# Softcap attention into a maxout MLP on one core: the second pair's k and q as f32 on the hardware queues, w_out first on GpSimd's queue, w1 in column halves

## The chip, the core and the metric

The kernel runs on one core of one Trainium2 chip. The core has five engines that work side by side, each through its own list of instructions in order: TensorE (PE: matmuls; PEld is its loading of weights), VectorE (DVE), ScalarE (ACT), GpSimd (POOL) and SyncE (SP). They wait for one another by semaphores. Data moves between the chip's main memory and the on-chip memory SBUF by DMA, which SyncE, ScalarE and GpSimd can issue; matmuls write to the accumulator memory PSUM. The metric is device time in microseconds (us) of one execution; lower is better.

## What is computed

```python
def _attn_ref(q, k, v, cap):                      # (8, 12, 448, 64) each, cap 30
    scale = 1.0 / np.sqrt(q.shape[-1])
    scores = scale * np.matmul(q, k.transpose(0, 1, 3, 2))
    scores = cap * np.tanh(scores / cap)
    scores = scores - np.max(scores, axis=-1, keepdims=True)
    attn = np.exp(scores)
    attn = attn / (np.sum(attn, axis=-1, keepdims=True) + 1e-09)
    return np.matmul(attn, v)

def _moe_ref(x, w1, w2, w_out):                   # x (3584, 768), w1, w2 (768, 1024), w_out (1024, 768)
    h1 = x @ w1
    h2 = x @ w2
    g = np.maximum(h1, h2)
    return g @ w_out
```

`x` is the attention's result with the heads side by side. All inputs and the output are f32.

## The kernel before

**Two pairs of formulas.** The maxout is rewritten as max(h1, h2) = relu(x (w1 - w2)) + x w2, so the result is relu(x wd) w_out + x wm with wd = w1 - w2 (`wd_sb`) and wm = w2 w_out (`wm_sb`). Both are made in the kernel, at its start: wd by subtractions on VectorE (step `sub`, L390), wm by "premultiplying" (`P`, L419), for which w2 is first turned by TensorE (`W`, L404) and copied out of PSUM (`WC`, L408).

**Attention, by pairs of heads.** The 8 x 12 heads make 48 pairs. The first ten pairs' k and q arrive as rows in `kqs` (two buffers of two pairs each), are turned by 28 transposes of 64 x 64 on TensorE (`X`, or `Xh` for one of its halves; L446) and copied to `qkT` (`XC`, L451). From pair 10 on a DMA transposes them (`cr`). Scores of a pair are three matmul groups (`S i j`, L502) into one of two score tiles in PSUM, s0 and s1; ScalarE takes the tanh out of them (`T`, L507) and then the exponential in SBUF (`E`, L524). The last 64 columns of two pairs share one tile (`L`, `TL`, `EL`). Sums of the exponentials (`Y`), their inverses (`Y1` to `Y3`) and the products with v (`VL`, `V`, L588 and L594) give `xT` (`N`, L606 and L609).

**The MLP.** 120 groups of matmuls (`M x y n`, L633) take `xT` with `wd_sb` (stage one, relu on VectorE, `ev`) and `xT`, `gT` with `wm_sb`, `wo_sb` (stage two), then the output is stored (`st`). A step of `M` works on two groups at once, one in each half of the array's rows; with -1 one half stays empty.

**The order of everything** is one list of steps, written out by hand or by a planner in the string `ORDER`; each step emits its instructions to their engines in that order, and nothing reorders them. So the order of each engine is the order of its steps in the list. `D bank n` is a filler: ceil(n / 4) matmuls of up to 512 columns on a tile of zeros (`warm`, L459), whose result is never read.

**The loads.** Only pair 0's k and q come as f32 over the hardware queues, k on SyncE's and q on ScalarE's (`ld0`, L303) and are cast to bf16 in `kqs`, k by VectorE, q by ScalarE (`cd`, L308 and L310). All others are cast on the way by GpSimd's DMAs: `lk`, `lq` (L321, one k or q of a pair), `lw2 c` (L370, one of six pieces of w2), `lwo half part` (L364, a quarter of w_out: one half of its columns, one half of its rows), `lv` (L352). `lw1 c` (L370) brings a piece of w1 in f32. Pieces 0 to 3 of w1 go to the output tiles `osb`, 4 and 5 to the second buffer of `xT`; w2 lies in the memory that `gT` takes later. GpSimd's DMAs use eight semaphores in turn, and each DMA waits until the one that last used its semaphore, the eighth before it, has landed.

**The lines that matter at the start**: fillers L459, transposes L446, scores L502 on TensorE; casts L308, L310; tanh L507; GpSimd's `identity` (L277), which writes the identity matrix that transposes need, over a tile that VectorE sets to zero (`ms0`).

Of the kernel before, what the change touches and what calls it, by code (L numbers as in the profile page):

```python
# [15 lines left out]
P 1 0 1; P 2 0 1; P 1 0 2; P 2 0 3; P 0 0 1; P 1 0 1; P 0 0 2; P 1 0 1; PC 2 0; EL 0; TL 1; E 1 0 2; T 2 0; EL 1;  # L16
S 3 0; S 2 2; T 3 0; T 2 2; Y 0 0; S 3 1; X 4 2; VL 0; V 0 1 0 2; V 0 0 0 3; V 0 1 2 3; P 0 0 1; T 3 1; E 2 0 3;
E 3 0 2; Y1 0; Y2 0; XC 4; PC 1 0; Y3 0; N 0 0; N 0 1; PC 0 0; OP 2 1 2; P 2 1 1; OP 0 1 1; P 0 1 4; OP 1 1 0;
P 1 1 1; P 2 1 1; P 1 1 1; P 2 1 2; P 1 1 2; S 3 2; S 4 0; P 0 1 1; P 1 1 1; P 0 1 3; P 1 1 1; OP 3 0 3; P 3 0 1;
P 2 1 1; P 3 0 1; P 1 1 2; T 3 2; T 4 0; E 3 2 3; PC 0 1; PC 1 1; S 4 1; S 4 2; X 5 1; Y 1 0; T 4 1; T 4 2; XC 5;  # L20
Y1 1; lk 8 0; lk 6 0; lq 8 0; lv 1 0; lq 7 0; lq 6 0; lw2 4; lw1 4; lv 5 2; lw1 0; lk 9 0; lw1 2; lv 2 1; lv 5 3;
lq 9 0; lv 2 0; L 2; P 2 1 1; W 5 1; VL 1; V 1 1 0 1; V 1 0 0 3; V 1 1 1 3; TL 2; E 4 0 3; S 5 0; X 6 0; P 2 1 2;
T 5 0; Y2 1; WC 5; Y3 1; N 1 0; N 1 1; PC 2 1; XC 6; P 3 0 4; S 5 1; S 5 2; P 3 0 1; OP 3 1 2; P 3 1 2; P 3 0 1;
W 4 0; P 3 1 4; EL 2; T 5 2; T 5 1; E 5 2 3; E 5 0 2; P 3 1 1; S 6 1; S 6 0; PC 3 0; WC 4; sub 4 0; T 6 1; T 6 0;
X 7 3; OP 4 0 0; P 4 0 5; P 3 1 1; lk 11 1; lw1 5; lw1 1; lw1 3; lv 3 1; lk 10 0; lv 3 0; lq 10 0; lk 10 1;
lk 11 0; lq 11 0; XC 7; sub 0 0; PC 3 1; P 4 0 1; Y 2 3; L 3; P 4 0 2; S 6 2; TL 3; T 6 2; Y1 2; Y2 2; Y3 2;
PC 4 0; sub 2 0; OP 5 0 3; P 5 0 3; S 7 0; X 8 2; X 9 0; VL 2; V 2 1 0 3; V 2 0 0 3; T 7 0; E 6 0 3; XC 9; XC 8;
N 2 1; N 2 0; sub 5 0; S 7 1; P 5 0 2; OP 5 1 2; P 5 1 2; OP 4 1 0; P 4 1 1; P 5 0 3; P 4 1 2; P 5 1 2; O 0 1;
M 0 -1 1; S 7 2; T 7 1; E 7 0 2; T 7 2; PC 5 0; sub 1 0; sub 3 0; S 8 0; P 5 1 4; P 4 1 4; S 8 1; O 1 3; M 1 -1 1;
T 8 0; T 8 1; M 1 -1 2; S 8 2; M 0 -1 5; L 4; Hs 0; cr 5; T 8 2; EL 3; TL 4; E 7 2 3; M 1 0 3; P 4 1 1; PC 5 1;  # L30
A 3 0 1; A 3 1 1; A 3 0 2; B 3 0; B 3 1; PC 4 1; A 3 1 2; VL 3; O 2 2; M 2 0 3; S 9 0; V 3 0 0 2; V 3 1 0 3;
V 3 0 2 3; Y 3 0; M 2 1 3; ev 0; Y1 3; Y2 3; Y3 3; Hs 2; T 9 0; EL 4; E 8 0 3; S 9 1; O 3 0; M 3 1 3; M 3 2 3;
O 4 1; M 4 2 1; Hs 3; M 4 2 2; M 4 3 3; ev 1; N 3 1; ev 2; N 3 0; T 9 1; E 9 0 2; Hs 4; O 5 3; M 5 3 3; M 5 4 3;
O 6 2; M 6 4 3; S 9 2; S 10 0; Hs 5; T 9 2; T 10 0; E 9 2 3; ev 3; M 6 5 3; Hs 6; O 7 0; M 7 5 3; M 7 6 3; S 10 1;
lq 12 0; lq 13 0; lk 13 1; lv 5 0; lk 12 0; lv 4 1; lk 12 1; lv 4 0; lv 5 1; lk 13 0; ev 4; A 4 0 1; A 4 0 2;
A 4 1 1; ev 5; Hs 7; cr 6; O 8 1; M 8 6 3; M 8 7 3; S 10 2; O 9 3; M 9 7 3; H 8; B 4 0; B 4 1; A 4 1 2; ev 6;
ev 7; T 10 1; T 10 2; M 9 8 2; L 5; VL 4; V 4 0 0 3; V 4 1 0 3; Y 4 2; TL 5; E 10 0 3; M 9 8 3; S 11 0; M 9 8 6;
O 10 0; M 10 8 3; Y1 4; Y2 4; Y3 4; N 4 1; N 4 0; Hs 9; Hs 8 2; T 11 0; EL 5; M 10 9 3; M 8 9 1; S 11 1; M 8 9 5;
S 11 2; M 8 9 2; lk 15 1; lq 14 0; lq 15 0; lk 14 0; lv 6 1; lk 14 1; lk 15 0; lv 6 0; lk 16 1; lk 16 0; lk 17 0;
lv 6 3; lv 6 2; lq 16 0; T 11 1; T 11 2; E 11 0 2; O 11 2; M 11 9 3; S 12 0; A 5 0 1; A 5 0 2; ev 8; ev 9;  # L40
M 11 10 7; S 12 1; lk 17 1; M 11 10 4; T 12 0; lq 17 0; O 12 1; M 12 10 1; A 5 1 1; M 12 10 1; Hs 11; cr 7;
M 12 10 1; M 12 11 1; B 5 0; M 12 11 1; T 12 1; M 12 11 1; S 12 2; H 10 2; B 5 1; M 10 11 1; T 12 2; M 10 11 5;
E 11 2 3; st 0 0; M 10 11 2; O 13 3; M 13 11 1; ev 10; L 6; VL 5; A 5 1 2; TL 6; V 5 0 0 2; V 5 1 0 2; Y 5 0;
# [16 lines left out]
TL 8; V 7 0 0 2; V 7 1 0 2; Y 7 3; E 16 0 3; V 7 0 2 3; lk 22 0; V 7 1 2 3; Y1 7; S 17 0; M 22 23 1; lv 9 0;  # L60
M 22 23 1; Y2 7; M 22 23 2; Y3 7; M 22 23 1; lv 9 1; M 22 23 2; O 25 3; M 25 23 1; N 7 0; M 25 23 1; lv 9 2;
# [20 lines left out]
O 38 3; M 38 36 1; A 10 1 1; M 38 36 1; Hs 37; cr 12; M 38 36 1; T 22 1; M 38 37 1; S 22 2; B 10 0; M 38 37 2;  # L82
T 22 2; O 39 2; M 39 37 1; ev 36; M 39 37 2; H 38; B 10 1; E 21 2 3; M 39 38 3; ev 37; L 11; VL 10; TL 11;
# [5 lines left out]
lq 29 0; M 41 40 1; T 24 0; M 41 40 1; A 11 1 1; O 42 3; M 42 40 1; cr 13; M 42 40 2; H 41; B 11 0; T 24 1;  # L89
M 42 41 1; S 24 2; M 42 41 2; H 40 2; B 11 1; M 40 41 1; T 24 2; M 40 41 5; st 2 0; E 23 2 3; M 40 41 2; O 43 2;  # L90
# [15 lines left out]
M 53 52 2; A 13 1 1; M 53 52 2; cr 15; M 53 52 1; T 28 1; M 53 52 1; B 13 0; S 28 2; M 53 52 2; B 13 1; O 54 3;  # L106
M 54 52 1; T 28 2; M 54 52 2; H 53; M 54 53 1; H 52 2; E 27 2 3; M 54 53 2; M 52 53 1; L 14; VL 13; A 13 1 2;
TL 14; V 13 0 0 2; V 13 1 0 2; Y 13 2; E 28 0 3; V 13 0 2 3; lk 34 0; V 13 1 2 3; Y1 13; S 29 0; M 52 53 1;
lv 15 0; M 52 53 1; Y2 13; M 52 53 2; Y3 13; M 52 53 1; lv 15 1; M 52 53 2; O 55 2; M 55 53 1; N 13 0; M 55 53 1;
lv 15 2; M 55 53 1; T 29 0; M 55 54 1; N 13 1; M 55 54 2; lv 15 3; M 55 54 2; EL 14; M 55 54 1; S 29 1; lk 34 1;  # L110
M 55 54 2; ev 52; M 55 54 1; T 29 1; S 29 2; lq 34 0; M 55 54 1; ev 53; M 55 54 1; O 56 0; M 56 54 1; T 29 2;
# [94 lines left out]
def kernel(  # L206
# [165 lines left out]
    def load_w2(c):  # L372
        load_rows(nc.gpsimd, w2b[:, c, :], moe_w2, c)
# [397 lines left out]
```

## Time and profile before

| what | us |
|---|---|
| median of 3 runs | 329.75 (329.73 to 330.23) |
| the profiled execution, device time | 330.89 |
| its span, first to last instruction | 329.1 |
| TensorE busy | 321.2 (98%) |
| ScalarE busy | 280.6 (85%) |
| VectorE busy | 240.5 (73%) |
| GpSimd busy | 161.6 (49%) |
| queue 0 (GpSimd's DMAs), 25.25 MB, share of 16 engines' span | 78.5% |
| queue 1 (SyncE's DMAs), 19.77 MB | 31.1% |

The page divides the span into 40 slices; TensorE's granted clock is full in all of them (mean 0.997). A busy TensorE isn't a TensorE at its peak, since ends of matmuls are modelled and fillers count as busy. Idle time of an engine in a row of the timeline stands in brackets with what ended it. A row such as "4.19 0.56 ACT L310 CAST" gives the start and the length in us, the engine, the line and the operation.

### The profile page before, as it was taken

How to read it: one execution, taken by the hardware profiler on the slowest of the kernel's cores; microseconds unless marked ns; L12 is line 12 of the kernel's file. 1: busy time of each engine (PE TensorE's matmuls, PEld its weight loads, DVE VectorE, ACT ScalarE, POOL GpSimd, SP SyncE). 2: the span in 40 equal slices, each digit the busy share in tenths (PEclk: the TensorE clock that was granted, in tenths of full speed). 3: DMA queues.
4: the chain of work that ended last, by engine and by line, in shares of the span. 5: the costliest groups of instructions: out<-in, count | busy, mean ns of one | idle time of the engine just before them, and what ended most of it. 6: DMA issues, size and time to landing. Idle time of an engine off the chain costs nothing.

```text
span 329.1 us, 9769 instructions
## 1 busy us (share of the span) xinstructions
PE 321.2 (98%) x4136; PEld 184.3 (56%) x4138; DVE 240.5 (73%) x422; ACT 280.6 (85%) x276; POOL 161.6 (49%) x239
## 2 busy tenths in 40 slices
PE   7899999999999999999999999999999999999995
PEld 3445453555646655555665565556466556557662
DVE  2327899996887878977897688878878879873201
ACT  3989999999999999999999999999999999921120
POOL 8266673757853863744783483585558211000000
PEclk9999999999999999999999999999999999999998
DMA  8999999999999999989999999989999963013033
GB/s 148 169 176 189 279 251 123 100 135 107 213 186 112 99 208 188 114 80 160 173 184 96 179 141 180 146 83 175 180 169 91 213 160 47 2 50 98 0 98 96
DMA packets 134507, 46.05 MB, mean 140 GB/s; under 512 B 112320, under 2 KB 129472, under 8 KB 134464
## 3 DMA queue, kind: packets, MB, share of 16 engines
q0 software_dynamic: 94880, 25.25, 78.5%
q1 hardware_dynamic: 39280, 19.77, 31.1%
q8 instruction: 32, 0.52, 0.6%
q10 hardware_dynamic: 304, 0.43, 0.4%
q14 instruction: 11, 0.09, 0.1%
HBM read 47.78 MB, written 11.01 MB: 179 GB/s over the span
## 4 chain that ended last, share of the span: by engine, by line
PE 90%; DMA 4%; DVE 3%; POOL 2%; issue 0%; POOLq 0%; DVEq 0%
PE mm L633 60%; PE s L502 9%; PE s L594 9%; PE mm L419 4%; DMA wo_sb<-in_moe_w_out_dram 4%; PE s L516 2%; PE mm L561 2%; PE s L588 1%; PE mm L628 1%; DVE wd_sb L390 1%; POOL kqs L321 1%; PE mm L446 1%; DVE esum L536 1%; POOL gT L370 1%; PE mm L554 1%; DVE wm_sb L425 0%
## 5 line engine op out<-in xcount | busy, mean ns | idle before, releaser
L507 ACT ACTIVATE e<-s 128x896 bf16<-128x896 f32 x144 | 125.2, 924 | 7.5 <-PE s L502 7.3
L524 ACT ACTIVATE e<-e 128x1792 bf16<-128x1792 bf16 (+2 forms) x72 | 122.5, 1706 | 0.1
L633 PE MATMUL mm<-wo_sb,gT 64*128 64x384 bf16 x864 | 115.1, 323 | 0.0
L633 PE MATMUL mm<-wm_sb,xT 64*128 64x384 bf16 x648 | 102.3, 323 | 0.0
L633 PE MATMUL mm<-xT,wd_sb 64*128 64x448 bf16 x768 | 97.1, 349 | 0.0
L328 POOL DMA_DIRECT2D kqs<-in_k_dram x76 | 54.6, 720 | 58.6 <-DMA qkT<-kqs 50.0
L633 PEld LDWEIGHTS <-gT 64*128 64x128 bf16 x864 | 58.5, 94 | 25.8 <-issue 0.7
L633 PEld LDWEIGHTS <-wd_sb 64*128 64x128 bf16 x768 | 48.9, 94 | 26.6 <-issue 2.0
L633 PEld LDWEIGHTS <-xT 64*128 64x128 bf16 x648 | 50.4, 94 | 19.0 <-issue 0.3
L502 PE MATMUL s<-qkT 64*128 64x448 bf16 x288 | 51.9, 352 | 0.6 <-ACT e L507 0.4
L352 POOL DMA_DIRECT2D vp<-in_v_dram x48 | 30.4, 638 | 34.3 <-PE s L502 22.9
L658 DVE TENSOR_SCALAR gT<-mm 128x448 bf16<-128x448 f32 x64 | 38.8, 617 | 8.7 <-PE mm L633 7.6
L328 POOL DMA_DIRECT2D kqs<-in_q_dram x38 | 35.0, 922 | 1.9 <-DMA osb<-in_moe_w_dram 1.7
L594 PE MATMUL s<-e,vp 128*32 128x448 bf16 x576 | 35.4, 354 | 0.0
L536 DVE TENSOR_TENSOR esum<-e 128x896 bf16<-128x896 bf16 x42 | 25.8, 617 | 10.0 <-ACT e L524 10.0
L609 DVE TENSOR_TENSOR xT<-s,inv 64x448 bf16<-64x448 f32 x48 | 29.9, 622 | 1.1 <-PE s L594 0.2
L536 DVE TENSOR_TENSOR esum<-esum,e 128x896 bf16<-128x896 bf16 x42 | 26.2, 624 | 5.9 <-ACT e L524 4.8
L502 PEld LDWEIGHTS <-qkT 64*128 64x128 bf16 x288 | 18.4, 94 | 20.8 <-issue 12.5
L692 ACT COPY osb<-mm 128x384 f32<-128x384 f32 x10 | 4.8, 478 | 26.9 <-PE mm L633 26.7
L541 DVE TENSOR_TENSOR esum<-esum,el 64x896 bf16<-64x896 bf16 x42 | 26.0, 619 | 1.5 <-PE mm L633 0.3
L694 DVE COPY osb<-mm 128x384 f32<-128x384 f32 x44 | 23.3, 554 | 5.2 <-PE mm L633 4.7
L566 DVE STREAM_TRANSPOSE st<-mm 128x448 f32<-128x448 f32 x24 | 15.6, 649 | 13.3 <-PE mm L561 11.4
(56 smaller groups left out, 269.5 us busy)
## 6 DMA issues: line engine op xcount, KB each, us to landing
out_dram<-osb SPq DMA_DIRECT2D x54, 192.0 KB, 5.0
vp<-in_v_dram POOLq DMA_DIRECT2D x38, 160.0 KB, 4.1
kqs<-in_q_dram POOLq DMA_DIRECT2D x47, 112.0 KB, 5.8
kqs<-in_k_dram POOLq DMA_DIRECT2D x76, 56.0 KB, 4.1
osb<-in_moe_w_dram POOLq DMA_DIRECT2D x4, 512.0 KB, 7.0
gT<-in_moe_w_dram POOLq DMA_DIRECT2D x6, 256.0 KB, 7.6
wo_sb<-in_moe_w_out_dram POOLq DMA_DIRECT2D x4, 384.0 KB, 9.6
vp<-in_v_dram POOLq DMA_DIRECT2D x10, 128.0 KB, 6.1
```

What stands on the lines that cost most here:

```text
L328: nc.gpsimd.dma_start(out=to, in_=x)
L352: nc.gpsimd.dma_start(out=to, in_=x)
L502: scored[i, j] = nc.tensor.matmul(s[:, h, :S], k_of(t, o, h, j), q_of(t, o, h)).ins
L507: nc.scalar.activation(expo[i][:, 2 * j : 2 * j + 2, :], slots[i, j][:, :, :S], AF.Tanh, scale=scale / cap)
L524: nc.scalar.activation(e, e, AF.Exp, scale=float(cap))
L536: nc.vector.tensor_add(d, e[:, 0:2, :] if j == 1 else d, e[:, 2 * j : 2 * j + 2, :])
L541: nc.vector.tensor_add(d, d, left_e[t][r, :, :])
L594: nc.tensor.matmul(vals[t][place(m, u), u, :S], w[:, m, :], expo[2 * t + o][:, 2 * j + h, :], start=False, stop=(j == NJ - 1))
L609: nc.vector.tensor_mul(x[64 - r : 128 - r], vals[t][r : r + 64, u, :S], sums[t, 3][64 - r : 128 - r])
L633: ins = nc.tensor.matmul(self.ps, w[r], x[r], start=first, stop=self.at == [self.n, self.n]).ins
L658: nc.vector.tensor_relu(gT[b // 2][:, f, cs], ps)
L694: nc.vector.tensor_copy(o[:, hs], ps)
```

## The change

The first 430 or so steps of `ORDER` are written anew; the last 1,908 are the same but for the PSUM bank that a group takes (2 and 3 change places). The first lines of the order before and after:

```diff
-ld0 k; ld0 q; ms0; ms; dm; cd k; D 3 16; lq 1 0; lk 2 0; lq 2 0; lk 1 0; lw2 3; id; lw2 2; lw2 1; lq 3 0; lw2 0;
-lk 3 0; lwo 0 0; lwo 0 1; cd q; D 3 16; Xh 0 0 0; Xh 0 1; XCh 0 0; XCh 0 1; D 3 8; S 0 0; T 0 0; S 0 1; D 3 16;
-S 0 2; X 1 1; D 3 23; W 3 2; T 0 1; T 0 2; XC 1; WC 3; S 1 2; L 0; D 3 16; X 2 2; D 3 4; E 0 0 3; T 1 2; TL 0;
-D 3 2; W 2 0; S 1 0; W 1 3; E 1 2 3; T 1 0; XC 2; S 2 1; S 1 1; X 3 2; W 0 1; T 2 1; T 1 1; lk 5 0; lk 4 0;
-lq 4 0; lk 7 0; lv 0 1; lv 0 0; lwo 1 0; lwo 1 1; lv 1 1; lw2 5; lq 5 0; WC 1; WC 2; XC 3; WC 0; S 2 0; L 1;
-OP 2 0 0; P 2 0 1; OP 1 0 1; P 1 0 1; P 2 0 1; OP 0 0 3; P 0 0 1; P 1 0 1; P 0 0 1; P 1 0 1; P 0 0 2; P 2 0 2;
...
+ld0 q; ld0 k; ms; ms0; dm; cd k; ld0 q 1; ld0 k 1; id; lwo 0 0; lw2 3; lw2 2; lk 3 0; lq 3 0; lw2 1; lk 2 0;
+lq 2 0; cd q; D 3 24; Xh 0 0 0; Xh 0 1; cd k 1 1; cd q 1 1; XCh 0 1; XCh 0 0; D 3 4; X 1 1; S 0 0; S 0 1; D 0 5;
+XC 1; T 0 0; T 0 1; D 1 16; S 0 2; L 0; W 3 2; T 0 2; TL 0; D 1 22; S 1 0; S 1 2; D 3 1; W 2 3; EL 0; T 1 0;
+T 1 2; lwo 0 1; lq 4 0; lk 4 0; lw2 0; lv 0 0; lv 0 1; WC 3; WC 2; D 2 8; S 1 1; D 2 4; OP 3 0 3; P 3 0 4; X 3 3;
+D 1 8; D 2 2; W 1 2; D 1 2; OP 2 0 1; P 2 0 2; XC 3; X 2 3; WC 1; XC 2; P 2 0 2; OP 1 0 2; P 1 0 3; S 2 1; T 1 1;
+E 0 0 3; E 1 0 2; T 2 1; S 2 0; P 1 0 2; P 3 0 1; P 1 0 1; P 3 0 1; L 1; P 2 0 1; P 1 0 2; P 2 0 2; P 3 0 2;
...
```

So pair 1's k and q (`ld0 q 1`, `ld0 k 1`) leave GpSimd's queue for the hardware queues and are both cast by ScalarE (`cd k 1 1`, `cd q 1 1`); pair 1's transposes (`X 1`) come ahead of the first scores; GpSimd starts with the identity and a quarter of w_out; premultiplying (`P`) starts before the pieces 1 and 0 of w2 are turned.

The code that goes with it:

```diff
-    def load_first(what):
-        raw[what] = stage.tile([P, S], f32, name=what + "r", bufs=1)
+    def load_first(what, i=0):
+        raw[what, i] = stage.tile([P, S], f32, name=what + "r", bufs=2)
         eng = nc.sync if what == "k" else nc.scalar
-        eng.dma_start(out=raw[what], in_=rows7(SRC[what], 0))
+        eng.dma_start(out=raw[what, i], in_=rows7(SRC[what], i))

-    def cast_first(what):
+    def cast_first(what, i=0, act=None):
         o = 0 if what == "k" else S
-        if what == "k":
-            nc.vector.tensor_copy(rows_of(0)[:, o : o + S], raw[what])
+        if act or (act is None and what == "q"):
+            nc.scalar.copy(rows_of(i)[:, o : o + S], raw[what, i])
         else:
-            nc.scalar.copy(rows_of(0)[:, o : o + S], raw[what])
+            nc.vector.tensor_copy(rows_of(i)[:, o : o + S], raw[what, i])
...
-    w2b = (
-        xpool.tile([P, FC, 2 * S], bf16, name="gT", bufs=1)
-        .rearrange("p f s -> p (f s)")[:, : KC * DF]
-        .rearrange("p (c n) -> p c n", c=KC)
-    )
+    w2b = const.tile([P, KC, DF], bf16, name="w2b")
...
+    HF = DF // 2
+
+    def load_w1(c):
+        place_w1(c)
+        n = slice(c % 2 * HF, (c % 2 + 1) * HF)
+        nc.gpsimd.dma_start(
+            out=w1_in[c].rearrange("p (u n) -> p u n", u=2),
+            in_=moe_w1.rearrange("(q p u) n -> q p u n", p=P, u=2)[c // 2][:, :, n],
+        )

     def subtract(c, eng):
-        eng.tensor_sub(wd_sb[:, c, :], w1_in[c], w2b[:, c, :])
+        n = slice(c % 2 * HF, (c % 2 + 1) * HF)
+        cs = slice(c // 2 * 2, c // 2 * 2 + 2)
+        eng.tensor_sub(wd_sb[:, cs, n], w1_in[c].rearrange("p (u n) -> p u n", u=2), w2b[:, cs, n])
```

A piece of w1 was one of six row blocks with all 1,024 columns; it is now one of two column halves of two row blocks. Pieces 4, 2 and 0 hold all rows of the first half, 5, 3 and 1 of the second; the order loads and subtracts 4, 2 and 0 first. w2 gets memory of its own. The new functions for w2 in f32 (`lr`, `cw`) are in no step of the order.

More of the change, by code (lines that the diff above doesn't have):

```diff
@@ L20 @@
[L20 to L34, printed above, removed]
@@ L366, in load_wo, with load_raw_w2, cast_w2 @@
         )
-    def load_rows(eng, to, w, c):
-        eng.dma_start(out=to, in_=w.rearrange("(q p u) n -> q u p n", p=P, u=2)[c // 2, c % 2])
     def load_w2(c):
-        load_rows(nc.gpsimd, w2b[:, c, :], moe_w2, c)
+        nc.gpsimd.dma_start(out=w2b[:, c, :], in_=moe_w2.rearrange("(q p u) n -> q u p n", p=P, u=2)[c // 2, c % 2])
+    raw_w2 = {}
+    def load_raw_w2(c, eng):
+        raw_w2[c] = stage.tile([P, DF], f32, name="w2r", bufs=1)
+        (nc.scalar if eng else nc.sync).dma_start(
+            out=raw_w2[c], in_=moe_w2.rearrange("(q p u) n -> q u p n", p=P, u=2)[c // 2, c % 2]
+        )
+    def cast_w2(c, act):
+        if act:
+            nc.scalar.copy(w2b[:, c, :], raw_w2[c])
+        else:
+            nc.vector.tensor_copy(w2b[:, c, :], raw_w2[c])
     w1x = xpool.tile([P, NP, 2 * S], bf16, name="xT").rearrange("p c s -> p (c s)").bitcast(f32)
@@ L643, in hand_over @@
             tc.add_manual_dep(self.turn, self.last[1].name, BANK, reason="bank")
-    def hold(i, j):
-        tc.add_manual_dep(nc.sync.nop().ins, scored[i, j].name, BANK, reason="order")
     def stage1(b, f):
@@ L723 @@
         "ld0": load_first, "cd": cast_first, "ms": lambda: [fill_const(nc.vector, i) for i in range(VB)],
[L724 to L725 removed]
+        "lk": lambda i, x: load("k", i, x), "lq": lambda i, x: load("q", i, x), "lkq": lambda t: load_quad("k", t), "lqq": lambda t: load_quad("q", t), "lw2": load_w2, "lr": load_raw_w2, "cw": cast_w2, "lwo": load_wo,
+        "lv": load_v, "lw1": load_w1, "sub": lambda c, e: subtract(c, nc.gpsimd if e else nc.vector),
         "cr": cross, "X": transposes, "XC": keep_qkT, "D": keep_warm, "dm": lambda: nc.vector.memset(warm, 0.0),
```

169 lines of the change are left out of this document (89 added, 80 removed).

## The prediction

> **What bounds the kernel now.** The page's head comes first, then the windows, the timeline and the waits.
>
> ```profile
> span 329.1 us, 9769 instructions
> ...
> PE 321.2 (98%) x4136; PEld 184.3 (56%) x4138; DVE 240.5 (73%) x422; ACT 280.6 (85%) x276; POOL 161.6 (49%) x239
> ```
>
> TensorE is busy for 321.2 of 329.1 us; no edit can win more than the 7.9 us of idle time plus the filler matmuls on `warm`. Where these lie is read from the windows (window, length, then busy us of PE, PEld, DVE, ACT, POOL, granted clock, DMA share, GB/s).
>
> ```profile
> 2.60:3.40 0.80, 0.80 (x3) 0.30 (x2) 0.00 (x0) 0.00 (x0) 0.80 (x2) 1.00 1.07 394
> 4.40:5.20 0.80, 0.80 (x3) 0.14 (x1) 0.01 (x1) 0.35 (x1) 0.80 (x3) 1.00 0.80 74
> 10.00:17.00 7.00, 5.66 (x78) 3.15 (x76) 2.77 (x5) 6.97 (x8) 1.20 (x3) 1.00 1.16 175
> 24.00:31.00 7.00, 7.00 (x100) 3.50 (x89) 5.34 (x10) 7.00 (x7) 3.29 (x6) 1.00 1.22 185
> 60.00:285.00 225.00, 225.00 (x2942) 131.70 (x2939) 187.62 (x331) 218.44 (x210) 127.33 (x180) 1.00 1.27 142
> ```
>
> From 10 to 17 us TensorE is idle for 1.3 us while the DMA engines are full (share over 1). From 24 us on TensorE and ScalarE are both full; from 60 us TensorE has no gap and ScalarE 3% of one. So two things can be moved: how soon the data comes, and how soon ScalarE, full from 8 to 60 us, gets scores. The timelines of PE and ACT show the start.
>
> ```profile
> 1.86 3.59 PE L459 MATMUL mm<-warm 128*128 128x512 bf16 x8 [1.86 <-DVE warm L726]
> 5.38 0.95 PE L446 MATMUL mm<-ident,kqs 64*64 64x64 bf16 x28
> 7.12 0.55 PE L502 MATMUL s<-qkT 64*128 64x448 bf16 x4 [0.24 <-DVE qkT L451]
> ...
> 4.19 0.56 ACT L310 CAST kqs<-qr 128x448 bf16<-128x448 f32 x1 [1.71 <-DMA qr<-in_q_dram]
> 7.53 2.54 ACT L507 ACTIVATE e<-s 128x896 bf16<-128x896 f32 x3 [2.77 <-PE s L502]
> 18.92 0.92 ACT L520 ACTIVATE el<-s 128x896 bf16<-128x896 f32 x1 [0.68 <-PE s L516]
> 23.40 2.54 ACT L507 ACTIVATE e<-s 128x896 bf16<-128x896 f32 x3 [0.33 <-PE s L502]
> ```
>
> Eight fillers, the first pair's transposes, its scores; then ScalarE runs with gaps of 0.68 and 0.33 us only. The waits on DMA:
>
> ```profile
> PE mm L446 <- DMA kqs<-in_k_dram: 0.9, 1, 0.9
> POOL wo_sb L364 <- DMA wo_sb<-in_moe_w_out_dram: 1.1, 1, 1.1
> ...
> L364 POOL DMA_DIRECT2D wo_sb<-in_moe_w_out_dram x1: 807/807/807, 7.1 to 7.1; - x1
> DMA to landing us min/median/max: 11.8/11.8/11.8
> ```
>
> The last two lines say that w_out, issued at 7.1, lands at 18.9, when the first premultiply can start. Issue plus landing gives all arrivals: q1 4.6, k2 6.1, q2 6.7, k1 7.2, four pieces of w2 8.7, 11.7, 14.0 and 16.7, q3 14.6, k3 17.0, w_out 18.9 and 21.1, then k and q about 0.55 apart. The GpSimd queue delivers one after the other: 0.55 us for a k or q, 1.45 to 3.05 for a piece of w2, 1.9 to 2.1 for one of w_out.
>
> **The change part by part.** *What stays.* The last 1,908 of 2,338 steps are the same but for bank numbers. They begin just before S 12 0, which runs at 75.3 us; half-array steps of the MoE part (M with -1) are 9 in both, and all other matmuls are equal in number. So the difference is what the first 75 us gain or lose, in TensorE and in ScalarE.
>
> *Fillers* go from 26 matmuls (101 units of 128 columns) to 27 (96). Of these the first run falls from 8 to 6; they start 0.43 apart (3.59 us for 8), so transposes of pair 0 can begin at 4.5 instead of 5.38, just after k's cast (4.01 + 0.39). That 0.9 us is free only as far as the next step is ready.
>
> *Second pair.* k1 and q1 leave the GpSimd queue, become 229 KB of f32 each behind k0 and q0, and cost ScalarE two casts of 0.56 us (row L310). Its gap from 4.75 to 7.53 covers these; without it they would be 1.1 us of ScalarE. The second DMA issue on ScalarE's queue (0.42) stands ahead of its table load (1.28), which then ends at 2.9, before qr at 4.1: 0. The new order puts the transposes X 1 ahead of the first scores. When k1 and q1 land at L, the casts end at L + 1.2, q's 14 transposes and the change of tile shape take 0.4, and S 0 0 starts at L + 1.6, against 7.12. Break-even is L = 5.5. The trace shows no second pair of such loads, so both ends: kr and qr, 459 KB, are through at about 3.5 (38, 75 and 315 KB moved to 3.4) and land at 3.9 and 4.1; 459 KB more at the 394 GB/s of the second window take 1.2 us, and with 0.5 to land L is 5.2. At the 74 GB/s seen in the third, up to 5.2 us, and 174 GB/s after it, L is 7.2. I take 5.2, since nothing else is in the queues until w_out starts near 4.3. S 0 0 then starts at 6.8 and ScalarE's first tanh at 7.2 instead of 7.53: 0.35 earlier. Behind X 1 wait all scores, and for these ScalarE.
>
> *The GpSimd queue.* Its first instruction is now the identity, which waits for VectorE's memset (about 1.6) and takes 0.44; the first DMA moves from 1.24 to 2.15. A first transfer landed 3.4 after issue, 0.55 of it its own. With 2.0 for w_out that is 7.0. Between q1 (4.6) and k2 (6.1) the queue lost 0.95 beyond k2's 0.55, at the 74 GB/s above. Whether this comes again the trace can't say: 0 to 0.95, and I take half, so w_out lands at 7.5. With w2 at the intervals seen: w2 8.95 and 12.0, k3 12.5, q3 13.1, w2 15.4, k2 15.9, q2 16.5, w_out 18.5, w2 21.7. Against before, one piece of w_out (2.0) has taken the place of one of w2 (2.1), and at 18.5 the same amount is in as before at 18.9. Every GpSimd DMA waits for the eighth before it, in both; the wait of 1.1 us above is this one, and both queues stay full.
>
> *TensorE until 19 us*, from these arrivals and the rows: X 1 5.9, first scores 6.8, S 0 2 8.6, w2's turn W 3 9.3 (w2 is there since 8.95), S 1 0 11.05, W 2 12.05, S 1 1 13.05, first four premultiplies 13.55, X 3 14.3, W 1 15.65 (w2 15.4), X 2 16.85, S 2 1 18.35. At 19.0 it has done 12 premultiplies (0.163 each by the chain, 2.0 us) and lacks L 1 and W 0 (0.9 us): 1.1 us ahead.
>
> *ScalarE* runs T 0 0 at 7.2, E 0 at 14.25, E 1 at 16.6 to 18.2, and waits 0.25 for S 1 1 and 0.5 for S 2 1, against 0.68 and 0.33 (above). Equal gaps, an earlier start: 0.35 us ahead. It is full until 60 us in both, so TensorE's other 0.75 us is lost again as waits for free score tiles; what reaches S 12 0 is ScalarE's 0.35.
>
> *w1 in column halves* keeps 512 KB a piece; 256 rows of 2 KB replace 128 of 4 KB. w1's pieces landed 1.05 to 2.0 apart. Issue could rise from 0.54 to w_out's 0.8 at most (512 rows): 6 x 0.26 = 1.6 us of GpSimd, idle half the span. Six subtractions of 1.2 us remain, but the first four column blocks need only three: M 0 and M 1 can begin earlier. Value 0, bounds -0.3 and, if each piece took 2.3 us, +2. w2 in its own tile removes a wait that no row shows: 0.
>
> *Sum.* -0.35 us. The profiled execution took 330.9 us (329.1 span, 1.8 around); it would be 328.75 and 330.55. The median of 329.75 lies 1.15 below that execution, so the forecast is 329.4.
>
> The Trainium skill (DMA: Bandwidth & Descriptors, "Issuing engines are not separate DMA queues") says that loads started from several engines share the same 16 DMA engines, and save only issue time. By that the moved loads win nothing in transfer; the trace agrees so far as 459 KB at 394 GB/s (1.2 us) and two GpSimd k/q transfers (1.1 us) cost alike, which is the third rival below.
>
> **The rivals.** *A: the queue's early loss does not come again*, because k1 and q1 fill that hole. w_out lands at 7.0 and everything behind 0.5 sooner; S 2 1 no longer makes ScalarE wait 0.5. 0.35 + 0.5: 328.9. For it: 74 GB/s right after 4 us, with only one queue active. Against: the hole stood behind GpSimd's first transfer and may move with it.
>
> *B: X 1 at the head holds the first scores.* If L is 6.2 (between 5.2 and 7.2, the second pair at half the rate, sharing with w_out), q1's cast ends at 7.4 and S 0 0 starts at 7.8, 0.7 late; ScalarE, full until 60 us, carries it, less 0.1 by the smaller gap at S 2 1: 330.35. It decides from L = 5.5. For it: the third window, and two casts in a row on ScalarE. Against: both hardware queues start at 0.74, long before w_out.
>
> *C: the transfers are hidden anyway.* What the earlier start gains, the identity ahead of GpSimd's first DMA (0.9 later) takes away at S 2 1: 329.75, no change.
>
> **How the numbers follow.** Forecast 0.42, A 0.25, B 0.25, C 0.08. The forecast's own range is 329.0 to 329.8 (k1 and q1 at 4.9 to 5.4, half the hole 0.2 to 0.8). Measurement tells 0.2%, 0.66 us, from no change. Faster by more: A and 0.08 of the forecast, 0.33. Within: 0.30 of it and C, 0.38. Slower: B and 0.04, 0.29. The range 328.6 to 330.7 reaches past A and B and leaves out the worst L and slow w1 pieces.
>
> **What would show it.** Right: k1 and q1 land by 5.4; the first tanh at 7.2; w_out's first piece by 7.5; TensorE at work on premultiplies before 14 us, and waiting for ScalarE between 33 and 54 us; S 12 0 at 74.9. Wrong: the first tanh after 7.6, an idle TensorE ahead of X 1, gaps at the second w2 piece, or a stage-one matmul waiting for VectorE's subtractions near 60 us.

## The result, and the profile after

| kernel | median of runs, us | lowest to highest | ratio to before, 95% interval |
|---|---|---|---|
| before | 329.74 (16 runs) | 329.00 to 330.85 | |
| after | 330.36 (16 runs) | 330.06 to 330.86 | 1.0018 (1.0010 to 1.0026) |

The change made the kernel slower by 0.6 us, 0.18%. Yet the profiled execution of after is 0.4 us *shorter* than the one of before: 330.47 us with a span of 328.7, against 330.89 and 329.1. The head of after's page:

```profile
span 328.7 us, 9775 instructions
...
PE 321.4 (98%) x4139; PEld 185.1 (56%) x4139; DVE 240.5 (73%) x422; ACT 281.4 (86%) x278; POOL 161.8 (49%) x237
```

TensorE's and ScalarE's start in the timeline of after (start, length, engine, line, operation, idle time before it and what ended it):

```profile
4.63 0.95 PE L458 MATMUL mm<-ident,kqs 64*64 64x64 bf16 x28
6.06 0.95 PE L458 MATMUL mm<-ident,kqs 64*64 64x64 bf16 x28
6.95 0.93 PE L514 MATMUL s<-qkT 64*128 64x448 bf16 x4
13.67 0.81 PE L431 MATMUL mm<-wo_sb,w2T 128*128 128x384 bf16 x4
39.58 0.32 PE L431 MATMUL mm<-wo_sb,w2T 128*128 128x384 bf16 x1 [0.37 <-DVE qkT L463]
50.10 0.36 PE L514 MATMUL s<-qkT 64*128 64x448 bf16 x2 [0.61 <-DVE xT L621]
...
7.54 1.73 ACT L519 ACTIVATE e<-s 128x896 bf16<-128x896 f32 x2 [1.53 <-PE s L514]
9.46 0.92 ACT L519 ACTIVATE e<-s 128x896 bf16<-128x896 f32 x1 [0.19 <-PE s L514]
18.82 1.73 ACT L519 ACTIVATE e<-s 128x896 bf16<-128x896 f32 x2 [0.32 <-PE s L514]
44.31 0.92 ACT L532 ACTIVATE el<-s 128x896 bf16<-128x896 f32 x1 [0.45 <-PE s L528]
50.51 2.54 ACT L519 ACTIVATE e<-s 128x896 bf16<-128x896 f32 x3 [0.50 <-PE s L514]
```

The transposes of pair 0 and then of pair 1 run where the prediction put them, the first premultiplies at 13.67, and the first tanh comes at 7.54, as in before. What was not foreseen stands in the last rows of each engine: TensorE waits twice for VectorE, at 39.6 and 50.1 us, and ScalarE twice for scores, 0.45 us at 44.3 and 0.50 us at 50.5. The windows of after show the same (window, length, busy time of PE, PEld, DVE, ACT, POOL, granted clock, DMA share, GB/s):

```profile
10.00:17.00 7.00, 6.83 (x80) 3.41 (x78) 2.62 (x4) 6.97 (x8) 4.02 (x7) 1.00 1.24 203
24.00:31.00 7.00, 7.00 (x86) 3.57 (x78) 4.91 (x9) 7.00 (x7) 4.77 (x8) 1.00 1.24 201
60.00:285.00 225.00, 225.00 (x2946) 131.96 (x2940) 188.04 (x332) 219.07 (x211) 126.96 (x179) 1.00 1.21 143
```

From 10 to 17 us TensorE is idle for 0.17 us instead of 1.34, and the transfers move 203 GB/s instead of 175. So the stretch that the change aimed at did become fuller, and the time still rose.

**One table for all that follows.** ScalarE's idle time is added up from its rows (gaps over 0.05 us) between the first tanh and the first tanh of pair 12, from where both kernels do the same. The median stands for all timed runs of a kernel, the other columns for its one profiled execution.

| profile | first tanh | gaps to 20 us | 20 to 60 | from 60 on | tanh of pair 12 | span | median |
|---|---|---|---|---|---|---|---|
| before, the recorded one | 7.53 | 0.68 | 0.43 | 0.64 | 77.21 | 329.1 | 329.74 |
| before, second | 7.53 | 0 | 0 | 0.65 | 76.07 | 327.9 | |
| before, third | 7.29 | 0 | 0.26 | 0.64 | 76.33 | 328.2 | |
| after | 7.54 | 0.51 | 0.95 | 0.06 | 76.78 | 328.7 | 330.36 |
| after, second | 7.35 | 0.86 | 0.94 | 0.06 | 77.20 | 329.2 | |
| a_s7 | 7.18 | 1.20 | 0.94 | 0.06 | 77.38 | 329.3 | 330.68 |
| a_s7_w5 | 6.83 | 0.67 | 0.50 | 0.06 | 76.08 | 328.0 | 330.47 |
| a_v2_w5 | 6.75 | 1.14 | 0.12 | 0.06 | 76.08 | 328.0 | 329.75 |
| a_nofill | 7.53 | 0.18 | 0.95 | 0.06 | 76.33 | 328.3 | 329.86 |
| a_three | 7.57 | 0 | 0.12 | 0 | 75.41 | 327.3 | 328.85 |
| a_four | 6.82 | 0.47 | 0.13 | 0.59 | 75.99 | 327.9 | 329.10 |
| a_w2first | 7.32 | 0.43 | 0.95 | 0.05 | 76.51 | 328.4 | 330.17 |
| a_x1late | 6.78 | 1.67 | 0.95 | 0.06 | 77.41 | 329.4 | 331.17 |
| a_kq1 | 7.35 | 1.55 | 0.95 | 0.06 | 77.89 | 329.7 | 332.43 |
| b_hw | 7.17 | 0 | 0.09 | 0.65 | 75.77 | 327.7 | 329.79 |
| b_nofill | 7.53 | 0 | 0.28 | 0.64 | 76.40 | 328.2 | 330.17 |

In every row the tanh of pair 12 minus the first tanh and the gaps leaves 67.6 to 68.1 us, ScalarE's own work, and the span minus that tanh is 251.8 to 252.0. So in these sixteen profiles an execution's time follows from the first tanh and ScalarE's gaps, to within about half a us: these two are what a kernel's order changes.

### The profile page after: what moved, and what is told of

It is laid out like the page before. It is cut to its first block, busy times and chain, and to the rows that moved or that the text cites. A ratio compares the mean times of both kernels' runs of the same rounds, so it can differ in the third digit from the quotient of the medians.

```text
span 328.7 us, 9775 instructions
## 1 busy us (share of the span) xinstructions
PE 321.4 (98%) x4139; PEld 185.1 (56%) x4139; DVE 240.5 (73%) x422; ACT 281.4 (86%) x278; POOL 161.8 (49%) x237
## 4 chain that ended last, share of the span: by engine, by line
PE 96%; DVE 2%; issue 0%
PE mm L645 61%; PE s L514 10%; PE s L606 9%; PE mm L431 4%; PE s L528 2%; PE mm L471 2%; PE mm L573 2%; PE s L600 2%; PE mm L640 1%; PE mm L458 1%; PE mm L416 1%; DVE xT L621 1%; PE mm L566 1%; DVE xT L618 0%; DVE qkT L463 0%
## 5 line engine op out<-in xcount | busy, mean ns | idle before, releaser
L514 PE MATMUL s<-qkT 64*128 64x448 bf16 x288 | 52.8, 355 | 0.6 <-DVE xT L621 0.6
```

What stands on the lines that cost most here:

```text
L514: scored[i, j] = nc.tensor.matmul(s[:, h, :S], k_of(t, o, h, j), q_of(t, o, h)).ins
```

## The experiments

The names: `a_` is the changed kernel with an edit, `b_` the kernel before with an edit. The mark that the first three expectations call the first tanh of pair 12 (73.9 and 73.5) is another row of the tanh's line, 3.3 us ahead of it; both move alike, and the table has the right one.

**Two more profiles of before, one of after**, with no edit.

> The kernel before, unchanged, profiled a second time. The changed kernel's profile has the step S 12 0 (the first of the steps that both kernels share) 0.42 us earlier than the recorded profile of before, and its span is 0.4 us shorter, yet its median is 0.6 us longer. Theory P (the recorded profile of before is an execution that lost about 1.1 us which a typical one does not lose): this profile has a span near 328.0 and S 12 0's tanh about 1.1 us earlier than in the recorded profile, near 72.8 instead of 73.9 for the first tanh of pair 12, with one shorter wait before 60 us to show for it. Rival Q (the difference lies around the span, in starting and ending the kernel): span 329.1 and the first tanh of pair 12 at 73.9 again, and the time 1 us shorter than span + 1.8. Rival R (the shared part after 75 us varies): first tanh of pair 12 at 73.9, and a span near 328.

> The kernel before, unchanged, profiled a third time, to see how far its executions lie apart. P: as in the second profile, first tanh of pair 12 between 72.6 and 73.9, span minus that time 255.2 in each. Q: 73.9 and 329.1. R: 73.9, and a span that differs by up to 1 us.

> The changed kernel, unchanged, profiled a second time. Its 16 times lie between 330.06 and 330.86, closer together than those of before (329.0 to 330.85). P: first tanh of pair 12 at 73.2 to 73.7 and a span of 328.3 to 328.8, as in its first profile (73.5, 328.7): the changed kernel is typical there. R: 73.5 and a span of 328 or 329.3.

Theory P holds: 1.14 and 0.88 us less at pair 12, spans of 327.9 and 328.2. ScalarE's timeline in the second profile of before has no bracket from 7.53 to 63 us:

```profile
7.53 2.54 ACT L507 ACTIVATE e<-s 128x896 bf16<-128x896 f32 x3 [2.76 <-PE s L502]
...
18.25 0.92 ACT L520 ACTIVATE el<-s 128x896 bf16<-128x896 f32 x1
...
22.42 2.54 ACT L507 ACTIVATE e<-s 128x896 bf16<-128x896 f32 x3
...
63.34 1.73 ACT L507 ACTIVATE e<-s 128x896 bf16<-128x896 f32 x2 [0.32 <-PE s L502]
67.99 0.92 ACT L520 ACTIVATE el<-s 128x896 bf16<-128x896 f32 x1 [0.32 <-PE s L516]
```

The gaps of 0.68 and 0.33 that the prediction read at 18.9 and 23.4 us are not there. TensorE's rows say why: pair 3's transposes, which waited 0.85 us for k3 in the recorded profile (first row), wait 0.17 in the second profile (second row).

```profile
17.06 0.63 PE L446 MATMUL mm<-ident,kqs 64*64 64x64 bf16 x28 [0.85 <-DMA kqs<-in_k_dram]
...
16.39 0.63 PE L446 MATMUL mm<-ident,kqs 64*64 64x64 bf16 x28 [0.17 <-DMA kqs<-in_k_dram]
```

So before's recorded execution carried 1 us of late data that the other two don't have; 13 of the 16 timed runs of before lie under 330 us, so most executions don't have it. The second profile of after is at 329.2, 0.5 above the first: after's own scatter was taken too small (328.3 to 328.8).

**a_s7: a wait of TensorE taken away.**

```diff
-lv 3 0; S 7 2; O 0 3; M 0 -1 3; S 7 1; M 0 -1 3;
+lv 3 0; O 0 3; M 0 -1 3; S 7 2; S 7 1; M 0 -1 3;
```

> The changed kernel with one step moved: S 7 2, which made TensorE wait 0.61 us at 50.1 us for VectorE's normalisation of V 2, stands behind the three stage-one matmuls M 0 -1 3 that followed it. Theory N (the changed kernel loses to a typical execution of before by waits of TensorE for VectorE that the new order has at 39.6 and 50.1 us; TensorE is the bound, so they go into the time one for one): the wait shrinks to about 0.05 and the time falls by 0.5 us, to 329.8, ratio to before 1.0000. Rival V (ScalarE is the bound from 8 to 60 us and waits 0.5 us at the same place for the same scores; TensorE's wait is covered): no change, 330.35, ratio 1.0018. Rival W (the loss is in the first 20 us or in w1's column halves): the wait goes and turns up later, ratio 1.0015 to 1.0020.

330.68 us, ratio 1.0030 (1.0018 to 1.0042): not better, and 0.3 above after, which the two intervals allow. Theory N falls, and two rows of this run bear out V:

```profile
50.03 0.74 PE L645 MATMUL mm<-xT,wd_sb 64*128 64x448 bf16 x3
...
51.11 2.53 ACT L519 ACTIVATE e<-s 128x896 bf16<-128x896 f32 x3 [0.50 <-PE s L514]
```

TensorE now works where it waited, but S 7 2 can't come before VectorE has emptied its tile, and ScalarE's gap is still 0.50 us. So it is ScalarE's gap, not TensorE's, that is taken as the bound up to 60 us from here on.

**a_s7_w5: the other wait as well.**

```diff
-OP 4 0 2; P 4 0 1; W 5 1; S 6 1;
+W 5 1; OP 4 0 2; P 4 0 1; S 6 1;
```

> As the run before, and in addition W 5 1 ahead of OP 4 0 2 and P 4 0 1, which waited 0.37 us at 39.6 us for VectorE's copy XC 8. N: both waits go, 330.36 - 0.95 = 329.4, ratio 0.999, and TensorE has no idle time from 17 us to S 12 0 but some 0.1 us. V and W: 330.35, ratio 1.0015 or more.

330.47, ratio 1.0019 (1.0010 to 1.0029). In the profile the gap of 0.45 at 44.3 us is gone (20 to 60 us: 0.50 left), as theory G, formed after this, says: the wait at 39.6 us delays L 3, and through it ScalarE. The medians of this run and the one before differ by 0.2 us, less than either interval's half-width (0.3 and 0.4 us). Against after's 330.36 there is no gain at all, where 0.45 us less of gaps should give 329.9. So the 0.45 is shown in the trace only, and these medians do not bear theory G out.

**a_nofill: no fillers behind S 0 2.**

```diff
-S 0 2; L 0; W 3 2; T 0 2; TL 0; D 1 22; S 1 0;
+S 0 2; L 0; W 3 2; T 0 2; TL 0; S 1 0;
...
-WC 3; WC 2; D 2 8; S 1 1; D 2 4; OP 3 0 0; P 3 0 4; X 3 3; D 1 8; D 2 2; W 1 2; D 1 2; OP 2 0 1;
+WC 3; WC 2; S 1 1; OP 3 0 0; P 3 0 4; X 3 3; W 1 2; OP 2 0 1;
```

> The changed kernel without the filler matmuls that stand behind S 0 2 (46 units of 128 columns, 2.8 us of TensorE between 10.1 and 16.6 us in the first profile); what is computed is the same. In that stretch TensorE has next to no idle time, so the fillers either cover waits for data or are on the path. Theory F (they are on the path from the landing of w2's first piece on: a late W 3 passes its 0.4 us to everything behind it): S 2 1 runs 1.0 to 2.5 us earlier than at 18.4, ScalarE's gaps at 12.2 and 18.8 go (0.3 to 0.8 us), and the time falls by 0.3 to 1 us. Rival C (they cover waits for w2, q2 and w_out, as laid out by the order): idle time of 2.5 us or more appears in their place, S 2 1 stays near 18.4, the time within 0.2 us of 330.36. Rival K (the granted or effective clock falls when TensorE idles): matmuls of 512 columns take 0.43 us instead of 0.21 in places and the time rises.

329.86, ratio 0.9997 (0.9987 to 1.0007): 0.5 us won, theory F. ScalarE's gap of 0.32 at 18.8 us is gone, and the tanh there comes at 18.36. The idle time that appears instead is TensorE waiting for ScalarE (0.95 us at 11.2, 0.90 at 19.3): it now runs ahead.

```profile
11.21 0.55 PE L514 MATMUL s<-qkT 64*128 64x448 bf16 x4 [0.95 <-ACT el L532]
...
18.36 1.73 ACT L519 ACTIVATE e<-s 128x896 bf16<-128x896 f32 x2
```

In this profile matmuls stay at their pace. But rival K is not out: two of the ten runs have a mean granted clock of 0.992 and 0.995, while no run of before or after whose clock is on record is under 0.997. The run a_four below shows what that is. (The lines of the order printed ahead of the prediction have `OP 3 0 3` where the kernel has `OP 3 0 0`, as here.)

**b_hw: the hardware-queue loads alone, in before.**

```diff
-ld0 k; ld0 q; ms0; ms; dm; cd k; D 3 16; lq 1 0; lk 2 0; lq 2 0; lk 1 0;
+ld0 k; ld0 q; ms0; ms; dm; cd k; ld0 k 1; ld0 q 1; D 3 16; lk 2 0; lq 2 0;
...
-lwo 0 1; cd q; D 3 16; Xh 0 0 0;
+lwo 0 1; cd q; cd k 1 1; cd q 1 1; D 3 16; Xh 0 0 0;
```

> The kernel before with one part of the change alone: k1 and q1 in f32 on the hardware queues, cast by ScalarE ahead of the first scores; the rest of the order stays, X 1 behind S 0 2 too. The GpSimd queue loses two transfers of 0.55 us, so w2, k3 and w_out land 1.1 us sooner. Typical executions of before already show ScalarE without a gap from 7.5 to 60 us and TensorE idle for 0.4 to 0.56 us between 10 and 17 us. Theory N (a typical execution of before has nothing left to win there except its scatter): no slower, at most 0.3 us faster, 329.45 to 329.75, and the times closer together than 329.0 to 330.85, since the wait for k3 at 17 us that cost the recorded profile 1 us can't come. Rival H (the part as such costs, by two casts of 0.56 us on ScalarE or by contention in the first 5 us): first tanh 0.3 us or more later than 7.53 and the time 0.3 us or more longer.

329.79, ratio 1.0006 (0.9995 to 1.0017). H is out: the first tanh is at 7.17, not later, and two casts on ScalarE cost nothing that can be told. But no gain can be told either, and the runs scatter as before's do (329.02 to 330.81). In the old order the loads are hidden, to within the interval of 0.4 us.

**a_v2_w5: both later gaps of ScalarE.** W 5 as above, and

```diff
-O 1 0; M 1 -1 1; S 7 0; VL 2; V 2 0 0 3; V 2 1 0 3; OP 5 0 2;
+O 1 0; VL 2; V 2 0 0 3; V 2 1 0 3; M 1 -1 1; S 7 0; OP 5 0 2;
```

> Moving S 7 2 took TensorE's wait of 0.61 us away and nothing from the time; so ScalarE, not TensorE, is taken as the bound from the first tanh to 60 us, and the time follows ScalarE's gaps (theory G). In the changed kernel these are 0.45 us at 44.3 (it waits for L 3, late by TensorE's wait for the copy XC 8) and 0.50 us at 50.5 (it waits for S 7 2, last of the chain tanh of S 6 2, values V 2, VectorE's normalisation, S 7 2), besides some 0.2 to 0.8 us before 20 us. Here W 5 1 stands ahead of OP 4 0 2 and P 4 0 1, and V 2 ahead of M 1 -1 1 and S 7 0, so that V 2 starts 0.4 us sooner. G: both gaps fall to 0.1 or less, S 12 0 comes 0.8 us sooner for the same start, 329.6, ratio 0.9995. Rival T (TensorE is the bound behind 60 us, where before's ScalarE itself waits twice 0.32 us): the first 0.3 to 0.5 us count and the rest is lost again at 63 to 68 us, 329.9 to 330.1, ratio 1.0005 to 1.001.

329.75, ratio 1.0003 (0.9994 to 1.0012): theory G, within 0.15 us of its number. The two gaps fall from 0.95 to 0.12 us and the time by 0.61, the whole of what the change had lost. Neither of ScalarE's rows there has a bracket any more (after's are at 44.31 and 50.51):

```profile
43.99 0.92 ACT L532 ACTIVATE el<-s 128x896 bf16<-128x896 f32 x1
...
48.77 3.57 ACT L519 ACTIVATE e<-s 128x896 bf16<-128x896 f32 x4
```

(The expectation's "V 2" is the product with v for pairs 4 and 5; its normalisation by VectorE frees the tile that S 7 2 needs.)

**a_three: this and no fillers.**

> The edits of the run before and, with them, no fillers behind S 0 2 (46 units left out; what is computed is the same), which alone gave 329.86 against 330.36. G: the gains add, 329.86 - 0.85 = 329.0, ratio 0.9977, and ScalarE shows no gap over 0.2 us between 7.5 and 60 us. T: 329.4 to 329.7, ratio 0.999 to 1.000, with new gaps of ScalarE behind 60 us.

328.85, ratio 0.9978 (0.9967 to 0.9988). This version is faster than both kernels, by 0.9 and 1.5 us, and G's number is met. The two edits alone gave 0.61 and 0.50, together 1.1; the 0.4 us more lie within the intervals of the medians. Windows of this run:

```profile
17.00:31.00 14.00, 13.10 (x177) 6.70 (x173) 7.85 (x15) 14.00 (x14) 8.73 (x16) 1.00 1.28 202
...
45.00:60.00 15.00, 14.84 (x188) 7.20 (x188) 14.23 (x25) 14.88 (x16) 8.75 (x12) 1.00 1.36 182
```

ScalarE (fourth busy time) is full or nearly so, TensorE (first) has room, and this is the faster kernel; in after TensorE has hardly any room between 10 and 17 us (6.83 of 7 us) and ScalarE waits at 18.8.

**a_x1late: pair 1's transposes behind the first scores** (prediction's rival B).

```diff
-D 3 4; X 1 1; S 0 0; S 0 1; D 0 5;
+D 3 4; S 0 0; S 0 1; X 1 1; D 0 5;
```

> The changed kernel with X 1 behind S 0 0 and S 0 1 instead of ahead of them. Rival B of the prediction (X 1 at the head holds the first scores, 0.75 to 0.95 us of TensorE at its slow pace of 53 ns for a pair of transposes): the first tanh comes at 6.3 to 6.8 instead of 6.8 to 7.5, ScalarE, full until 60 us, keeps 0.4 us or more of it, and the time is 329.9, ratio 1.0005. Theory G with the fillers (what holds ScalarE near 12 and 19 us is TensorE, which runs without a gap from 4.6 us on and does the same work): the first tanh is earlier by 0.5 us or more, the gap ahead of S 1 0 (12.2 us) grows by as much, S 2 1 stays, and the time is 330.2 to 330.5.

331.17, ratio 1.0041 (1.0027 to 1.0054): neither. The first tanh is at 6.78, but ScalarE then waits 1.06 us for S 0 2, which stands behind four fillers (`D 1 16`), and these wait for the copy of X 1:

```profile
8.20 1.02 PE L471 MATMUL mm<-warm 128*128 128x512 bf16 x3 [0.34 <-DVE qkT L463]
...
9.56 0.92 ACT L519 ACTIVATE e<-s 128x896 bf16<-128x896 f32 x1 [1.06 <-PE s L514]
```

The fillers use PSUM bank 1, the bank of X 1's transposes. So with the fillers where they are, the early place of X 1 is an advantage. What X 1 at the head costs by itself this run can't say: X 1 late without these fillers was not tried.

**a_w2first: w2's first piece ahead of w_out's.**

```diff
-id; lwo 0 0; lw2 3; lw2 2;
+id; lw2 3; lwo 0 0; lw2 2;
```

> The changed kernel with w2's first piece ahead of w_out's on GpSimd's queue. In three of four profiles TensorE waited for this piece ahead of W 3, 0.39, 0.57 and 0.92 us, in one not at all, and what is behind it came later by as much. Theory L (w_out first makes w2 late, and the fillers leave no room to make it up): no wait ahead of W 3, S 2 1's tanh near 18.5 in every profile, 329.9, ratio 1.0005, and a smaller scatter. Rival M (what decides is only how early TensorE reaches its full pace, 5.4 to 7.5 us): the wait goes, the time stays at 330.2 to 330.5.

330.17, ratio 1.0016 (1.0007 to 1.0024). The wait ahead of W 3 is gone and W 3 runs at 9.41, and the median is 0.2 us lower, 0.4 of what theory L said. The intervals of this run and of after overlap, so L and M are not decided; if there is a gain, it is small.

**a_kq1: k1 and q1 back on GpSimd's queue, in the new order.**

```diff
-cd k; ld0 q 1; ld0 k 1; id; lwo 0 0;
+cd k; id; lq 1 0; lk 1 0; lwo 0 0;
...
-cd k 1 1; cd q 1 1;
```

> The changed kernel with k1 and q1 back on GpSimd's queue, cast by the transfer, behind the identity and ahead of w_out; ScalarE's two casts go. They land near 5.3 and 5.9, so X 1 starts near 6.1 as now; everything behind them on the queue lands 1.1 us later, w2's first piece at 10.2 to 11.3. Theory L (the moved loads are worth what they take off GpSimd's queue, since w2's first piece is late already): the wait ahead of W 3 grows by 0.7 to 1.1 us and the time with it, 331.0 to 331.5, ratio 1.004 to 1.005. Rival H (the loads are hidden anyway, as in the run that moved them in before: 329.79 against 329.73): 330.2 to 330.6, ratio 1.0015 to 1.0025.

332.43, ratio 1.0092 (1.0076 to 1.0109), 2.1 us above after, beyond either number. Its profile, the fastest of its executions (331.48), explains the first 1.1:

```profile
6.39 0.63 PE L458 MATMUL mm<-ident,kqs 64*64 64x64 bf16 x28 [0.55 <-DMA kqs<-in_k_dram]
10.78 0.62 PE L416 MATMUL mm<-ident,w2b 128*128 128x128 bf16 x8 [1.26 <-DMA w2b<-in_moe_w_dram]
```

TensorE waits for k1 and 1.26 us for w2. What the slower executions add was not profiled; the slowest (333.87) has a mean granted clock of 0.995, the others 0.997 and more.

**a_four: a_three with w2 first** (the edit of a_w2first).

> The version with three edits (V 2 and W 5 moved, no fillers behind S 0 2; 328.85) with w2's first piece ahead of w_out's on GpSimd's queue. Theory L: the wait ahead of W 3 (0.58 us in its profile) goes, S 1 0 waits only for ScalarE, and the time falls by 0.1 to 0.3 us, 328.55 to 328.75, ratio 0.9967. Rival: without fillers TensorE has 1.4 us of slack behind W 3 and makes up for it: 328.85, ratio 0.9978.

329.10, ratio 0.9981 (0.9972 to 0.9991): no gain over a_three, but not by the rival's reason. The wait moves to w2's second piece, 0.73 us ahead of W 2, and then TensorE works at half its pace: the eight transposes of a step W take 1.04 us at 11.8 and 0.62 again at 15.4.

```profile
11.79 1.04 PE L416 MATMUL mm<-ident,w2b 128*128 128x128 bf16 x8 [0.73 <-DMA w2b<-in_moe_w_dram]
...
15.40 0.62 PE L416 MATMUL mm<-ident,w2b 128*128 128x128 bf16 x8
```

The trace's record of the granted clock has one half from 11.76 to 15.17 us. This is rival K of a_nofill. Six of the twelve runs have such a clock (mean 0.992 to 0.995) and a median of 329.41; the other six (1.00) have 328.78, as a_three has 328.85. In a_three, with the same fillers left out, no run of eleven is under 0.998.

**b_nofill: before without its fillers behind S 0 2** (45 units; the expectation says 46).

```diff
-S 0 2; X 1 1; D 3 23; W 3 2;
+S 0 2; X 1 1; W 3 2;
...
-L 0; D 3 16; X 2 2; D 3 4; E 0 0 3; T 1 2; TL 0; D 3 2; W 2 0;
+L 0; X 2 2; E 0 0 3; T 1 2; TL 0; W 2 0;
```

> The kernel before without its fillers behind S 0 2 (46 units of 128 columns between 9.4 and 13.7 us left out; what is computed is the same). Theory G: in a typical execution of before ScalarE has no gap between 7.5 and 60 us, so the fillers cover waits and cost nothing: 329.6 to 329.8, ratio 1.0000, with TensorE idle where they stood. Rival F2 (fillers cost the time in both kernels): 329.2 to 329.4, ratio 0.9985. Rival K (the pace of TensorE falls where it idles): slower.

330.17, ratio 1.0012 (0.9995 to 1.0029), with runs from 329.0 to 331.9: no gain in the median. Where the fillers stood TensorE waits for ScalarE, which has no gap there:

```profile
14.20 0.37 PE L502 MATMUL s<-qkT 64*128 64x448 bf16 x2 [1.83 <-ACT el L520]
```

In before the fillers lie in TensorE's spare time; in after, with the new order, they lie on the path. The scatter goes with the clock, rival K again: eight of the twelve runs have a mean granted clock of 0.987 to 0.995 and a median of 330.5, the four others (0.997 and more) one of 329.46. So F2's 329.2 to 329.4 is not excluded where the pace holds, though four runs are few; what before's fillers are worth is that the pace does hold.

## Why the prediction was right and wrong

The forecast was 0.35 us faster than before, the measured median is 0.62 us slower. It lies inside the stated range of 328.6 to 330.7, but on the other side of before.

**The baseline: wrong, and the first failed step.** "The median of 329.75 lies 1.15 below that execution, so the forecast is 329.4" took these 1.15 us off as a constant of the execution. They were no constant: two more profiles show that they are the late k3 and its 0.68 and 0.33 us, the very gaps that the sum compared with. Against a typical execution of before there were no gaps of 1.0 us to set against the new ones. Counted against the recorded profile, the forecast was right to 0.1 us (span 328.75 forecast, 328.7 measured), and that is luck. By the table, the first tanh did not come earlier, the gaps from 20 to 60 us are 0.52 longer, those up to 20 us 0.17 and those behind 60 us 0.58 shorter, and ScalarE's own work is 0.22 shorter: 0.43 us at the tanh of pair 12, where 0.35 was forecast from the first tanh alone. The hint was in the times: 330.89 lay above all three given runs.

**The loads and the queue: right, and from w2's second piece on better than forecast.** k1's cast starts at 4.98 and q1's at 5.45 (forecast 5.2 for both landings). w_out's first piece is issued at 1.84 and lands 5.7 us later, at 7.6 (7.5). In after's profile w2's first piece lands at 9.1 (8.95), the second at 10.4 (12.0), k3 at 11.0 (12.5), q3 at 11.6 (13.1), w2's third at 12.8 (15.4), q2 at 15.1 (16.5). But across the executions w2's first piece lands between 9.1 and 10.3, and a late one moves what is behind W 3.

**The first tanh: 7.2 forecast, 6.75 to 7.57 measured** with one and the same head of the order. The forecast of 6.8 for S 0 0 was nearly met (6.95); then in after's profile the first four score matmuls took 0.93 us instead of 0.55, since TensorE was still at its slow pace. Transposes of pair 1 took 0.95 in this profile, and in the profile of a_v2_w5, with the same steps up to there, 0.73:

```profile
5.69 0.73 PE L458 MATMUL mm<-ident,kqs 64*64 64x64 bf16 x28
6.35 0.55 PE L514 MATMUL s<-qkT 64*128 64x448 bf16 x4
```

The prediction had no term for this; the last section has the moments.

**ScalarE's gaps to 20 us: right in size, wrong in what they meant.** 0.25 + 0.5 us were forecast, 0.51 and 0.86 measured. They were called equal to before's 0.68 and 0.33; before has none as a rule. And it was thought that TensorE would be 1.1 us ahead at 19 us: it worked with hardly a pause, some 2.5 us of it on the 46 units of fillers that a_nofill leaves out (0.21 us for four units), and reached S 2 1 at 18.41, as forecast (18.35), with ScalarE waiting. Taking them out gives 0.5 us.

**20 to 60 us: wrong, the second failed step.** "It is full until 60 us in both, so TensorE's other 0.75 us is lost again as waits for free score tiles." The walk through the order ended at 19 us, and the rest, although written anew, was taken as equal. The new order has two waits for VectorE there that reach ScalarE: P 4 0 1 behind the copy XC 8 (0.45 us at 44.3), and S 7 2 behind the normalisation of V 2 (0.50 at 50.5). Together 0.95 us, 0.83 of which a_v2_w5 takes away, and with them 0.61 us of the time; that each of the two counts by itself is shown by no median (a_s7, a_s7_w5). TensorE's waits for ScalarE between 33 and 54 us that were to show the forecast right are not in the profile.

**Behind 60 us: a gain that was not forecast.** Before's ScalarE waits twice 0.32 us near 63 and 68 us in all its profiles; in after this is 0.06. It is why 0.95 us and the start together cost only 0.6; what in the new order removes it was not tried.

**w1, w2's tile, the casts: 0, as said.** A piece of w1 costs GpSimd 0.73 us of issue instead of 0.54, and no wait of TensorE follows near 60 us. b_hw shows that the two casts cost nothing that can be told. w1's halves alone were not tried.

**The rivals.** A (the hole comes not again) agrees with the earlier k3 and w2, but its gain was not to be had, since before's typical execution doesn't have the wait either. B has the number (330.35 against 330.36) by luck: its L of 6.2 and S 0 0 at 7.8 were not measured (in after's profile both loads had landed by 5.23, S 0 0 came at 6.95), and moving X 1 back cost 0.8 us more, though by way of the fillers. C is nearest for the loads in the old order (b_hw). In the new order they are far from hidden: without them 2.1 us are lost.

**The sum by runs:** from the table's rows of before (second, third) and after (both), the first tanh is the same within 0.05 us in the mean, the gaps to 20 us add 0.69, those from 20 to 60 add 0.82, those behind 60 take 0.59 away, and ScalarE's own work is 0.16 shorter: +0.8 us at the tanh of pair 12, against +0.62 in the medians. Two profiles of one kernel lie 0.3 to 0.4 us apart there, so the two numbers agree as far as they can.

## What to carry to other kernels

Before a gap of a profile enters a sum, ask whether the median has it: a profiled execution 1 us above the median holds 1 us of something, and if the edit removes just that, it can't be won from the median. Then follow the engine whose gaps make the time (here ScalarE, though TensorE was 98% busy) through the whole stretch that was rewritten, not only the part that the edit was meant for. Fillers and early loads have no price of their own: about the same amount of fillers lies in spare time in one order and costs 0.5 us in the other, and the same two loads are worth nothing in one and 2 us in the other. And before fillers are taken out, look at the granted clock of all runs, not of the profiled one alone.

## What the runs showed of the hardware

TensorE starts slow and changes its pace at a moment that differs between executions: with the same first matmul at 1.86 us, transposes come at 53 ns a pair (28 in 0.95 us) or at 32 ns (0.63), and matmuls of 512 columns at 0.43 or 0.21 us. In b_hw the fast pace is there at 5.35 us,

```profile
5.35 0.63 PE L446 MATMUL mm<-ident,kqs 64*64 64x64 bf16 x28
```

in after not before some 7.3 us (its score matmuls from 6.95 on take 0.93 us instead of 0.55). The trace's record of the clock agrees: the full clock begins at 5.25 us in b_hw, at 7.86 and 6.98 in the two profiles of after, at 6.33, 6.93 and 5.62 in the three of before, and between 4.93 and 7.86 in all sixteen. Ahead of the first record the windows count the clock as full, so their 1.00 says nothing of the start. (Nor is the granted clock of before's page full in all slices: the last one reads 8 tenths.) With after's start of the order, the first tanh comes at 6.75 to 7.18 where the moment lies before 5.9 us (three profiles) and at 7.35 to 7.57 where it lies behind 6.9 (four).

The Trainium skill (TensorE: Matmul & The Clock Gate, "What's actually happening") says that TensorE runs at half its clock until a window of some 3.4 us has been busy, that the windows don't start with the kernel, and that the moment therefore varies by 500 ns to either side. The two paces agree, 1 to 2; here the moment lies 3.1 us behind the first matmul in one profile and 6.0 in another, a wider spread than that.

The full pace can be lost again. In a_four it is gone for 3.41 us from 11.76 us on; in the 3.41 us before, TensorE was busy for 1.83 us. In b_nofill's profile it was busy for 2.00 of the 3.42 us from 13.21 on and kept the full clock. Where between the two the limit lies, or whether busy time alone decides, these runs do not show.

The same transfer, issued at 2.72 us behind the same neighbours, landed between 9.1 and 10.3 us in eight profiles of kernels whose GpSimd queue starts alike. What makes it late stays open.
